# Copies and attention of the first batch a step later, in a kernel of top-k attention and Fourier mixing

## The chip, the cores and the metric

The kernel runs on one core of a Trainium2 chip. Its time is the device time of one execution in microseconds; the time before is the median of three runs. A core has five engines that run side by side and wait for each other by semaphores: TensorE (PE, with its weight loads as PEld), VectorE (DVE), ScalarE (ACT), GpSimd (POOL) and SyncE (SP), which issues transfers here. [...]

## What is computed

There are 8 batches with 8 heads, 576 tokens and a head size of 64. For each row of the scores, only the 32 largest stay, and the softmax is taken over them; its product with v is the attention's output. Per batch, the heads side by side make a 576 x 512 matrix x. It is mixed by a Fourier transform over both axes, normalised, and sent through two layers of weights:

```python
scores = scale * np.matmul(q, k.transpose(0, 1, 3, 2))
kth = np.partition(scores, -top_k, axis=-1)[..., -top_k:-top_k + 1]
scores = np.where(scores >= kth, scores, -1000000000.0)
...
mixed = np.real(np.fft.fft(np.fft.fft(x, axis=1), axis=2))
u = x + mixed
un = (u - mu) / np.sqrt(var + 1e-06)
return u + np.maximum(un @ w_ch1, 0.0) @ w_ch2
```

The weights arrive as 64-bit floats. The kernel reads them as pairs of 32-bit words and makes 32-bit floats of them itself.

## The kernel before

**Items and steps.** Two heads make a pair, four pairs a batch. The rows of a pair's scores are cut into nine items (`IN_PAIR`, L301): four row tiles of 128 for each head, and one item (e is None) with the 64 last rows of both heads. The main loop (L1394) has one step per item, 36 for a batch (`PER_BATCH`). Steps 1 to 36 are those of the first batch's items (`short`, L1399), in which no layer of the batch before can run yet.

**One item's way.** Its scores are made on TensorE three steps ahead (`scores`, L309: a large product of 128 x 512 per head, L369, and a small one for the last keys, L339), and ScalarE copies them to the tile S at once (L372, L343). VectorE finds the 32 largest in four rounds of MAX8 (L393) with three MATCH_REPLACE8 (L395) between. GpSimd makes two thresholds of them (`bounds`, L402). ScalarE's mask (L409) and a GpSimd subtraction (L412) turn the scores into what the exponential (L418, `expo`) needs. A step later TensorE transposes the result P in blocks of 128 (`transposes`, L439, L450) and ScalarE copies the blocks to PT (L442, L451). When a few items are there, `attend` (L476) multiplies PT with v; `attended` (L490, L502) copies the output and the sums; `to_tokens` (L516) transposes it back, and VectorE normalises it into x (L520).

**The weights.** During steps 1 to 33 of the first batch, 32 chunks of weights of 128 x 512 are converted, about one per step: ScalarE scales the high word (L191), converts the low word (L207) and takes the sign (L210); VectorE shifts the result by three bits (L199); GpSimd adds the low word (L218) and multiplies by the sign (L220). The plan (`at`, L1212) calls the ScalarE part "convert", the others "shift", "join" and "pool". Four column means of the first weights are taken on TensorE (`centre`, L1246, L1250), in steps 19, 27, 36 and 37; their copy by ScalarE (L1263) is under "convert" of the step after. GpSimd then subtracts them (L1259): for the first two one instruction in each of the four steps that follow.

**Order in a step.** It is written out by hand. ScalarE first runs "convert", then the exponential of the item before; then the list `fixed` is worked through: scores with their copies, query or key transposes for the next pair (`prep`, L269), attention's tokens, planned TensorE work, transposes of P with their copies, attention. Then the loads are issued on SyncE (`load_nat`, `load_v`), and VectorE's rounds, GpSimd's thresholds and the mask of the step's own item follow. In step 36 the attention of the last items is finished, and step 37 has VectorE fold x for the Fourier products (L631 to L586); the products over tokens (`dft_tokens`, L667), over channels (L724, L728) and the first layer (L878) follow.

**Buffers.** Score products and column means share two banks (`ps_s`); query, key and P transposes share two others (`ps_t`); attention and its tokens have one (`ps_o`), other work three (`ps_m`). A bank is free again when the copy out of it is done.

```python
        fixed.append(lambda: scores(j - 1, 1) if e == 1 else scores(j, 0))
        fixed += preps
...
            fixed.append(lambda: transposes(done))
...
        run(i, "convert")
        if short:
            expo(i - 1)
        for n, fn in enumerate(fixed):
            cost += fn()
...
        if i < PER_BATCH:
            mask(i, lambda: run(i, "join"))
```

Of the kernel before, what the change touches and what calls it, by code (L numbers as in the profile page):

```python
# [18 lines left out]
P = 128  # L19
# [53 lines left out]
def kernel(  # L73
# [234 lines left out]

    def scores(i, part):  # L309

# [21 lines left out]
        if part == 1:  # L332

            copy = nc.scalar.copy if i else nc.vector.tensor_copy
            shape, name = [P, NF * P], f"sp_{i}_t"
            sp = ps_s.tile(shape, F32, name=name, tag="sp") if i else bank(shape, name)

            q_end = P * t + rows
            nc.tensor.matmul(  # L339
                sp[:, 0:P], lhsT=qT[:, q_end - P:q_end], rhs=kt_t, start=True, stop=True  # L340
            )
            for h, (s_t, r, _, tails) in enumerate(to):
                copy(out=s_t[r, tails], in_=sp[P - rows:P, TAIL * h:TAIL * (h + 1)])  # L343
            return 0.3
        if e is None and i >= PER_BATCH:

            half = NF * P // 2
            sps = [
                ps_s.tile([P, NF * P], F32, name=f"sp_{i}_{h}", tag="sp") for h in range(2)
            ]  # L350
            for g in range(2):
                for h in range(2):
                    hd = slice(D * h, D * (h + 1))
                    nc.tensor.matmul(
                        sps[h][TAIL * g:TAIL * (g + 1), 0:half],
                        lhsT=qT[hd, q_cols], rhs=kT[hd, half * g:half * (g + 1)],
                        start=True, stop=True,
                    )
            for h, (s_t, r, _, _) in enumerate(to):
                for g in range(2):  # L360
                    nc.scalar.copy(
                        out=s_t[r, half * g:half * (g + 1)],
                        in_=sps[h][TAIL * g:TAIL * (g + 1), 0:half],
                    )
            return 0.6
        for h, (s_t, r, keys, _) in enumerate(to):
            hd = slice(D * h, D * (h + 1))
            sp = ps_s.tile([P, NF * P], F32, name=f"sp_{i}_{h}", tag="sp")
            nc.tensor.matmul(  # L369
                sp[r], lhsT=qT[hd, q_cols], rhs=kT[hd, :], start=True, stop=True  # L370
            )
            nc.scalar.copy(out=s_t[r, keys], in_=sp[r])  # L372
        return 1.04
# [48 lines left out]

    def transposes(i):

# [4 lines left out]
        if (pair, ch) not in PT:  # L429
            PT[pair, ch] = attp.tile(  # L430
                [P, 2 * NF + 1, CW[ch]], F32, name=f"PT_{pair}_{ch}", tag=f"PT{ch}", bufs=1
            )
        pt = PT[pair, ch]

        def full():
# [5 lines left out]
            for he, o, w in dsts:  # L441
                nc.scalar.copy(  # L442
                    out=pt[:, NF * he:NF * (he + 1), col:col + w], in_=tp[:, :, o:o + w]
                )

        def tails():
            tp = ps_t.tile([P, 4, P], F32, name=f"tpP_{i}_t", tag="tp")
            if e == 1:
                both = Wp.pop(i - 1).rearrange("p e s -> p (e s)")[:, NF * P:S + TAIL]
                nc.tensor.transpose(tp[:, 0, :], both, ident)  # L450
                nc.scalar.copy(out=pt[:, 2 * NF, col:col + P], in_=tp[:, 0, :])  # L451
                return
            Wp.pop(i)
            nc.tensor.transpose(tp[:, 0, :], p_sb[:, S - P:S], ident)
            nc.scalar.copy(out=pt[TAIL:P, 2 * NF, col:col + TAIL], in_=tp[TAIL:P, 0, TAIL:P])
            for r in (0, TH):
                nc.scalar.copy(
                    out=pt[r:r + TH, 2 * NF, col:col + TAIL],
# [892 lines left out]

    queue, waiting, pending, written, now, out_next = [], [], [], set(), [0], []
    step_us = 6.0

# [39 lines left out]
    while i < N + 4 or plan or queue or sums:  # L1394
# [9 lines left out]
        fixed, j = [], i + 3  # L1404
        e = items[j][2] if j < N else None
        preps = []
# [21 lines left out]
        for where in ("pe1", "pe2", "pe"):  # L1428
            fixed += plan.pop((i, where), [])
        if e is None and j < N:  # L1430
            fixed.append(lambda: scores(j, 1))
        n_tr = len(fixed)
        if done is not None:
            fixed.append(lambda: transposes(done))
        if short:
            fixed += tok
            pair, r = divmod(i - 1, PER_PAIR)
            piece = {1: (0, 0, P), 4: (0, P, CW[0]), 6: (1, 0, P), 8: (1, P, CW[1])}.get(r)
            if piece is not None:
                fixed.append(lambda: attend(pair, *piece))  # L1440
            if i == PER_BATCH:
                fixed.append(lambda: attended(NPB - 1, 1, late_next) or 0.0)
                fixed.append(lambda: to_tokens(NPB - 1, 1, False))
        if i in arrivals:
# [21 lines left out]
        if short:  # L1466
            if piece is not None and r in (4, 8) and i < PER_BATCH:

# [82 lines left out]
```

## Time and profile before

| | |
|---|---|
| time, median of three runs | 1907.32 us (1907.11 to 1907.42) |
| the profiled execution: its own time / span | 1907.16 us / 1905.4 us |
| TensorE busy, whole span | 1790.4 us (94%) |
| VectorE busy, whole span | 1585.3 us (83%) |
| ScalarE / GpSimd busy, whole span | 1208.5 / 908.4 us |
| mean granted TensorE clock | 0.969 |
| step of the first batch, between two threshold products (L402) | 5.42 us with a shift, 5.08 without |
| last threshold product of the first batch begins | 217.63 us |
| first product of the first layer (L878) begins | 255.88 us |

The span runs from the first to the last instruction; the execution's own time has a little more around it. A row of the timeline has start and duration in us, engine, line, operation, output<-inputs, shapes and count, and in brackets how long the engine had stood idle before it and what ended that. Where stretches are compared, each row has the stretch, its length, each engine's busy time in us with its count of instructions, the granted TensorE clock as a share of full speed, and the share of the DMA engines. Times from L402 mean: counted from the start of that item's threshold product.

### The profile page before, as it was taken

The numbers are of one execution on the slowest core, as the hardware profiler recorded it, in microseconds if no ns is written. First come the engines' busy times: TensorE is split into PE (matmuls) and PEld (weight loads), VectorE is DVE, ScalarE is ACT, GpSimd is POOL, SyncE is SP. The second block draws the span as 40 slices with busy tenths as digits, with TensorE's granted clock in tenths as the row PEclk, the third lists the DMA queues.
The fourth block names the chain that finished last, engine by engine and source line by source line (L and its number), as shares of the span: only waits on it lengthen the run. The fifth ranks groups of instructions, "written<-read, shape, count | busy, mean of one in ns | idle before, by whom it ended". The sixth has DMA issues, their size and how long they took to land.

```text
span 1905.4 us, 28704 instructions
## 1 busy us (share of the span) xinstructions
PE 1790.4 (94%) x9200; PEld 1182.4 (62%) x9200; DVE 1585.3 (83%) x3301; ACT 1208.5 (63%) x3078; POOL 908.4 (48%) x1278
## 2 busy tenths in 40 slices
PE   5567799999899999999999999999999999999999
PEld 3344465474567756667567656667567656667678
DVE  7999999999899999989899888989899888872110
ACT  6878657776766767657676667666676667652100
POOL 4768643556535374345534464245534464241022
PEclk7787899999999999999999999999999999999999
DMA  5333001311104111131113101141113102030132
GB/s 165 104 94 108 20 13 50 99 56 25 41 14 130 34 25 47 42 107 28 25 47 98 53 20 52 35 114 27 25 47 97 53 19 57 25 103 6 50 101 80
DMA packets 184342, 111.25 MB, mean 58 GB/s; under 512 B 125952, under 2 KB 174208, under 8 KB 184192
## 3 DMA queue, kind: packets, MB, share of 16 engines
q1 hardware_dynamic: 183408, 109.20, 20.3%
q8 instruction: 74, 1.21, 0.3%
q14 instruction: 76, 0.62, 0.1%
q10 hardware_dynamic: 784, 0.21, 0.0%
HBM read 93.63 MB, written 15.73 MB: 57 GB/s over the span
## 4 chain that ended last, share of the span: by engine, by line
PE 80%; ACT 8%; DVE 6%; POOL 3%; issue 1%; DMA 1%; SPq 1%; POOLq 0%; DVEq 0%; ACTq 0%
PE hp L878 26%; PE cp L905 10%; PE o L476 8%; PE tpP L439 6%; PE sp L369 5%; PE cw L1075 5%; PE cv L1075 4%; PE yp L667 3%; PE cp L944 3%; DVE m L393 2%; DVE wk L395 2%; PE sp_t L339 2%; PE mp L728 2%; POOL wk L412 1%; ACT wk L409 1%
## 5 line engine op out<-in xcount | busy, mean ns | idle before, releaser
L412 POOL TENSOR_TENSOR wk<-S,wk 128x576 f32<-128x576 f32 x288 | 407.7, 1416 | 731.8 <-ACT wk L409 701.2
L393 DVE MAX8 m<-wk 128x8 f32<-128x576 f32 x864 | 626.3, 749 | 6.1
L878 PE MATMUL hp<-unT,w 128*128 128x256 f32 (+1 forms) x2048 | 539.9, 410 | 2.6 <-ACT unT L796 2.6
L878 PEld LDWEIGHTS hp<-unT,w 128*128 128x128 f32 x2048 | 374.3, 191 | 124.7 <-issue 25.8
L395 DVE MATCH_REPLACE8 wk<-m,wk 128x576 f32<-128x576 f32 x576 | 427.6, 742 | 0.0
L418 ACT ACTIVATE wk<-wk,nt 128x576 f32<-128x576 f32 x288 | 224.7, 780 | 75.6 <-POOL wk L412 74.5
L409 ACT ACTIVATE wk<-S,nt 128x576 f32<-128x576 f32 x288 | 226.8, 787 | 36.2 <-POOL nt L402 35.2
L439 PE MATMUL tpP<-ident,wk 128*128 128x128 f32 x1152 | 183.9, 284 | 67.3 <-ACT wk L418 40.7
L905 PE MATMUL cp<-w,hT 128*128 128x512 f32 x512 | 240.6, 598 | 0.0
L442 ACT COPY PT<-tpP 128x512 f32<-128x512 f32 (+1 forms) x320 | 171.2, 547 | 106.8 <-PE tpP L439 104.3
L393 DVE MAX8 m<-S 128x8 f32<-128x576 f32 x288 | 214.0, 743 | 21.6 <-ACT S L343 21.6
L439 PEld LDWEIGHTS tpP<-ident,wk 128*128 128x128 f32 x1152 | 141.2, 145 | 141.2 <-ACT wk L418 64.2
L882 ACT ACTIVATE hT<-hp 128x320 f32<-128x320 f32 (+1 forms) x256 | 104.7, 409 | 194.5 <-PE hp L878 192.1
L395 DVE MATCH_REPLACE8 wk<-m,S 128x576 f32<-128x576 f32 x288 | 213.7, 742 | 0.0
L476 PE MATMUL o<-PT,v 128*64 128x256 f32 (+3 forms) x1440 | 195.2, 414 | 1.9 <-ACT PT L442 1.8
L372 ACT COPY S<-sp 128x512 f32<-128x512 f32 (+1 forms) x264 | 141.7, 588 | 48.9 <-PE sp L369 48.6
L369 PE MATMUL sp<-kT,qT 64*128 64x512 f32 (+1 forms) x528 | 160.2, 666 | 4.8 <-ACT means L1263 3.3
L476 PEld LDWEIGHTS o<-PT,v 128*64 128x64 f32 x1440 | 111.4, 152 | 73.8 <-issue 16.7
L905 PEld LDWEIGHTS cp<-w,hT 128*128 128x128 f32 x512 | 88.8, 190 | 86.3 <-issue 86.2
L1020 POOL TENSOR_TENSOR hT<-hT 128x512 f32<-128x512 f32 x64 | 81.4, 1275 | 100.3 <-ACT hT L882 88.6
L1075 PE MATMUL cw<-w,hT 128*128 128x256 f32 x448 | 106.7, 383 | 1.4 <-POOL nt L402 1.2
L1075 PEld LDWEIGHTS cw<-w,hT 128*128 128x128 f32 x448 | 81.4, 190 | 18.9 <-issue 5.2
(157 smaller groups left out, 2179.3 us busy)
## 6 DMA issues: line engine op xcount, KB each, us to landing
w<-w_parts SPq DMA_DIRECT2D x82, 512.0 KB, 4.4
space<-in_moe_w_ch_dram SPq DMA_DIRECT2D x32, 512.0 KB, 3.5
nat<-in_q_dram SPq DMA_DIRECT2D x128, 64.0 KB, 2.1
v<-in_v_dram SPq DMA_DIRECT2D x128, 64.0 KB, 2.2
out_dram<-x SPq DMA_DIRECT2D x32, 256.0 KB, 2.1
nat<-in_k_dram SPq DMA_DIRECT2D x124, 64.0 KB, 2.2
w_parts<-w_t SPq DMA_DIRECT2D x8, 512.0 KB, 2.9
w_s<-w_parts SPq DMA_DIRECT2D x8, 512.0 KB, 4.8
```

Source lines behind the costliest of these rows:

```text
L369: nc.tensor.matmul(sp[r], lhsT=qT[hd, q_cols], rhs=kT[hd, :], start=True, stop=True)
L393: ops.append(lambda src=src, m8=m8: nc.vector.max(out=m8, in_=src))
L395: ops.append(lambda src=src, m8=m8: nc.vector.match_replace(w, m8, src, NEG))
L409: nc.scalar.activation(out=w, in_=Ssb[i], func=AF.Relu, scale=-FAR, bias=Nt[i][:, 1:2])
L412: nc.gpsimd.tensor_tensor(out=w, in0=Ssb.pop(i), in1=w, op=ALU.subtract)
L418: nc.scalar.activation(out=w, in_=w, func=AF.Exp, bias=Nt.pop(i)[:, 0:1], accum_out=den_t[pair % 3][:, c:c + 1],)
L439: nc.tensor.transpose(tp[:, c, :], p_sb[:, k0 + P * c:k0 + P * (c + 1)], ident)
L442: nc.scalar.copy(out=pt[:, NF * he:NF * (he + 1), col:col + w], in_=tp[:, :, o:o + w])
L476: nc.tensor.matmul(o[D * e:D * (e + 1), c0:c1], lhsT=vv[:, c, e, :], rhs=pt[:, 2 * NF if c == NF else NF * e + c, c0:c1], start=(c == 0), ...
L878: nc.tensor.matmul(hp[:, 0:w], lhsT=w1[:, dt, P * it:P * (it + 1)], rhs=unT[:, dt, 0:w], start=(dt == 0), stop=(dt == NDT - 1),)
L905: nc.tensor.matmul(cp, lhsT=hT[:, it, P * n:P * (n + 1)], rhs=w2[:, it, :], start=(it == 0), stop=(it == NIT - 1),)
L1075: nc.tensor.matmul(dst, lhsT=h()[a][:, kc, :], rhs=rhs_of(kc), start=start and kc == 0, stop=kc == NK - 1, skip_group_check=True,)
```

## The change

In the first batch:

- Scores of an item are made four steps ahead (`next_scores(i + 4, held_s)`), behind the transposes of P, and their copies are kept in a list and issued at the beginning of ScalarE's next step. An item with e None makes its three score products in one step.
- The copies of P are kept likewise (`held`) and issued a step later, ahead of the exponential. Attention of an item's group runs a step later, after the scores; its tokens follow it.
- ScalarE's step begins with the scaling ("scale", L191 alone) and ends, ahead of the mask, with the rest of "convert" (L207, L210, and the copy of a column mean).
- The exponential stands in the list, behind the copies, the query or key transposes and the planned TensorE work, ahead of the transposes of P.
- In step 36 everything that ends the batch goes first: exponential, copies, transposes, attention, its copy and tokens; the held score copies, planned work (the third column mean) and the query transposes come after.

```diff
+    def copier(held):
+        if held is None:
+            return nc.scalar.copy
+        return lambda **kw: held.append(lambda: nc.scalar.copy(**kw))
...
-            nc.scalar.copy(out=s_t[r, keys], in_=sp[r])
+            copier(held)(out=s_t[r, keys], in_=sp[r])
...
-    def transposes(i):
+    def transposes(i, held=None):
...
+        copy = copier(held)
...
-        at(s0 + 1, "convert", lambda n=n: scale_high(n))
+        at(s0 + 1, "scale", lambda n=n: scale_high(n))
...
-        fixed.append(lambda: scores(j - 1, 1) if e == 1 else scores(j, 0))
+
+        def next_scores(j, held=None):
+            if e_of(j) == 1:
+                return scores(j - 1, 1, held)
+            t = scores(j, 0, held)
+            return t + scores(j, 1, held) if e_of(j) is None and held is not None else t
+
+        if 1 < i <= PER_BATCH:
+            begun_s = held_s[:]
+            held_s.clear()
+            fixed.append(lambda: [fn() for fn in begun_s] and 0.0)
+        else:
+            fixed.append(lambda: next_scores(j))
         n_mask = 0
-        fixed += preps
+        if i != PER_BATCH:
+            fixed += preps
...
-        if done is not None:
+        if done is not None and not short:
             fixed.append(lambda: transposes(done))
         if short:
-            fixed += tok
-            pair, r = divmod(i - 1, PER_PAIR)
+            begun = held[:]
+            held.clear()
+            last_of = i == PER_BATCH
+
+            def copies():
+                for fn in begun:
+                    fn()
+                return 0.0
+
+            tile = i - 1 if last_of else i - 2
+            pair, r = divmod(tile, PER_PAIR)
             piece = {1: (0, 0, P), 4: (0, P, CW[0]), 6: (1, 0, P), 8: (1, P, CW[1])}.get(r)
...
+            if last_of:
+                fixed[:] = [
+                    lambda: expo(i - 1) or 0.0, copies, lambda: transposes(i - 1), *pieces,
+                    lambda: attended(NPB - 1, 1, late_next) or 0.0,
+                    lambda: to_tokens(NPB - 1, 1, False), *fixed, *preps,
+                ]
+            else:
+                fixed.insert(1, copies)
+                fixed += [
+                    lambda: expo(i - 1) or 0.0, lambda: transposes(i - 1, held),
+                    lambda: next_scores(i + 4, held_s), *pieces, *tok,
+                    lambda: run(i, "convert") or 0.0,
+                ]
...
-        run(i, "convert")
-        if short:
-            expo(i - 1)
+        run(i, "scale")
+        if not short or last_of:
+            run(i, "convert")
```

More of the change, by code (lines that the diff above doesn't have):

```diff
@@ L307, with scores @@
     N = len(items)
-    def scores(i, part):
+    def copier(held):
+        if held is None:
+            return nc.scalar.copy
+        return lambda **kw: held.append(lambda: nc.scalar.copy(**kw))
+    def scores(i, part, held=None):
         if not 0 <= i < N:
@@ L332, in scores @@
         if part == 1:
-            copy = nc.scalar.copy if i else nc.vector.tensor_copy
+            copy = copier(held) if i else nc.vector.tensor_copy
             shape, name = [P, NF * P], f"sp_{i}_t"
@@ L360, in scores @@
                 for g in range(2):
-                    nc.scalar.copy(
+                    copier(held)(
                         out=s_t[r, half * g:half * (g + 1)],
@@ L441, in full @@
             for he, o, w in dsts:
-                nc.scalar.copy(
+                copy(
                     out=pt[:, NF * he:NF * (he + 1), col:col + w], in_=tp[:, :, o:o + w]
@@ L450, in tails @@
                 nc.tensor.transpose(tp[:, 0, :], both, ident)
-                nc.scalar.copy(out=pt[:, 2 * NF, col:col + P], in_=tp[:, 0, :])
+                copy(out=pt[:, 2 * NF, col:col + P], in_=tp[:, 0, :])
                 return
@@ L454, in tails @@
             nc.tensor.transpose(tp[:, 0, :], p_sb[:, S - P:S], ident)
-            nc.scalar.copy(out=pt[TAIL:P, 2 * NF, col:col + TAIL], in_=tp[TAIL:P, 0, TAIL:P])
+            copy(out=pt[TAIL:P, 2 * NF, col:col + TAIL], in_=tp[TAIL:P, 0, TAIL:P])
             for r in (0, TH):
-                nc.scalar.copy(
+                copy(
                     out=pt[r:r + TH, 2 * NF, col:col + TAIL],
@@ L1352 @@
     queue, waiting, pending, written, now, out_next = [], [], [], set(), [0], []
+    held, held_s = [], []
     step_us = 6.0
@@ L1404, with e_of @@
         fixed, j = [], i + 3
-        e = items[j][2] if j < N else None
+        def e_of(j):
+            return items[j][2] if j < N else None
+        e = e_of(j)
         preps = []
@@ L1429 @@
             fixed += plan.pop((i, where), [])
-        if e is None and j < N:
+        if e is None and j < N and not 1 < i <= PER_BATCH:
             fixed.append(lambda: scores(j, 1))
         n_tr = len(fixed)
-        if done is not None:
+        if done is not None and not short:
             fixed.append(lambda: transposes(done))
         if short:
-            fixed += tok
-            pair, r = divmod(i - 1, PER_PAIR)
-            piece = {1: (0, 0, P), 4: (0, P, CW[0]), 6: (1, 0, P), 8: (1, P, CW[1])}.get(r)
[L1439 to L1443, printed above, removed]
+            begun = held[:]
[7 more added lines that the diff above has]
+            pair, r = divmod(tile, PER_PAIR)
+            piece = {1: (0, 0, P), 4: (0, P, CW[0]), 6: (1, 0, P), 8: (1, P, CW[1])}.get(r)
+            piece = piece if tile >= 0 else None
+            pieces = [lambda: attend(pair, *piece)] if piece is not None else []
+            if last_of:
[11 more added lines that the diff above has]
+                ]
         if i in arrivals:
@@ L1466 @@
         if short:
-            if piece is not None and r in (4, 8) and i < PER_BATCH:
+            if piece is not None and r in (4, 8) and not last_of:
                 out_next.append(lambda pc=(pair, r // 8): attended(*pc, late_next))
```

## The prediction, made before the result was known

> **What bounds the kernel now.** I read the stages first (busy time of each engine in four stretches), then the one VectorE group of the first batch whose durations differ from one another, then the timeline around it, and last the timeline where the first batch ends. All rows are of the profiled execution (span 1905.4 us, own time 1907.16 us; the median of the runs is 1907.32 us, so a sum against this execution carries over to the median within 0.2 us).
>
> ```profile
> core 0: us, PE busy (x) PEld busy (x) DVE busy (x) ACT busy (x) POOL busy (x), PEclk, DMA share, GB/s
> 17.00:120.00 103.00, 63.47 (x327) 41.87 (x329) 101.48 (x209) 87.79 (x204) 73.46 (x71) 0.72 0.42 127
> 120.00:217.60 97.60, 65.82 (x323) 39.20 (x322) 94.89 (x193) 79.25 (x185) 76.98 (x72) 0.78 0.25 75
> 217.60:255.90 38.30, 32.42 (x208) 21.45 (x206) 37.22 (x88) 18.25 (x49) 12.06 (x28) 1.00 0.04 9
> 255.90:1905.00 1649.10, 1620.01 (x8321) 1076.20 (x8321) 1343.85 (x2789) 1017.49 (x2628) 744.55 (x1100) 1.00 0.19 53
> ```
>
> VectorE is busy 98.5% and 97.2% of the first batch and 97.2% of the change to the second, TensorE 98.2% of all that follows. So the change, which touches only the first batch, can act in two ways: VectorE's time up to 217.6 us, and the moment at which TensorE begins its unbroken work after 255.9 us. What is won or lost there shifts the end by as much, for what follows keeps its order and waits for no clock.
>
> VectorE hardly waits in the first batch. What it loses lies inside its own instructions, in the integer shift of a weight chunk (L199):
>
> ```profile
> L199 DVE TENSOR_SCALAR w<-w x32: 401/411/1403, 21.8 to 206.3; 128x512 int32<-128x512 int32 x32
> ```
>
> The group's busy time is 19.5 us where 32 times 0.41 would be 13.1: 6.4 us are stretching, in 11 of the 32 shifts. There is also one true wait, of 1.3 us (L199 for ScalarE's L191). One stretched shift in the timeline:
>
> ```profile
> 74.59 0.78 ACT L409 ACTIVATE wk<-S,nt 128x576 f32<-128x576 f32 x1
> ...
> 75.45 1.43 POOL L412 TENSOR_TENSOR wk<-S,wk 128x576 f32<-128x576 f32 x1 [1.65 <-ACT wk L409]
> ...
> 76.83 1.29 POOL L220 TENSOR_TENSOR w<-w,space 128x512 f32<-128x512 f32 x1
> ...
> 77.38 1.02 DVE L199 TENSOR_SCALAR w<-w 128x512 int32<-128x512 int32 x1
> ```
>
> The shift begins while GpSimd multiplies (76.83 to 78.12) and ends 0.28 us after it. GpSimd was late since ScalarE's mask (L409) was late: it began 2.46 us after the threshold product (L402, at 72.13) that it needs. A full step of VectorE is 5.42 us from one L402 to the next, and the next shift starts 5.26 us after it. Mask to L412 is 0.86, L412 to the end of L220 2.68. So a mask later than 5.26 - 2.68 - 0.86 = **1.72 us** after its L402 stretches the next shift, by as much as it is later, up to about 1.1.
>
> Then the end of the batch, on TensorE:
>
> ```profile
> 217.74 0.98 PE L283 MATMUL tpq<-ident,nat 128*128 128x128 f32 x5
> 218.56 3.60 PE L1250 MATMUL cm<-w,ones 128*128 128x512 f32 x8
> 222.15 0.66 PE L439 MATMUL tpP<-ident,wk 128*128 128x128 f32 x4
> ...
> 225.25 0.44 PE L516 MATMUL tpx<-ident,xT 128*128 128x128 f32 x2 [0.46 <-ACT xT L490]
> 225.62 0.87 PE L354 MATMUL sp<-kT,qT 64*64 64x256 f32 x8
> 227.32 3.70 PE L1250 MATMUL cm<-w,ones 128*128 128x512 f32 x8 [0.84 <-ACT S L361]
> ...
> 234.30 0.75 PE L667 MATMUL yp<-fs,fg 128*64 128x145 f32 x7
> ```
>
> The query transposes and the third column mean fill the 4.4 us in which TensorE would wait for the last softmax. Later it waits for VectorE's folds just once, so its slack there is 1.15 us:
>
> ```profile
> 239.83 0.46 PE L667 MATMUL yp<-fs,fsp 128*64 128x145 f32 x2 [1.15 <-DVE fsp L563]
> ```
>
> [...] 0.41 us for 512 elements alone, up to 1.40 beside GpSimd, ending 0.28 after GpSimd's instruction. [...] So a copy that waits holds the mask behind it; the 1.3 us wait is such a case (ScalarE stood 2.92 us for a score copy behind the first column mean).
>
> **The change part by part.** No instruction is added or removed; the order views of GpSimd and SyncE are the same row by row, those of TensorE, ScalarE and VectorE differ only up to the batch's end. VectorE's difference is each normalisation a step later: nothing, as it has no wait there and its inputs come a step earlier than it.
>
> *Copies of P and scores a step later, scaling first, conversion last.* ScalarE's step becomes: scaling (L191), score copies, copies of P, query or key copies, exponential, L207 and L210, mask. It no longer waits for transposes or scores of its own step. In a plain step, counted from L402: mask at 0.33, L191 at 1.02, copies from 1.58 to 3.0 (two score copies 0.94, one of P 0.48), exponential when GpSimd's L412 is done, 0.33 + 0.86 + 1.5 = 2.7 or 3.13 behind L218, 0.87 for it, 1.12 for the two conversions: free at 5.13, the next mask wanted at 5.75. So a plain step has 0.62 + 1.39 = 2.0 us before a shift is stretched. That removes the plain cases (32.7, 54.6, 77.4, 105.6 us: 1.9 us in all) and the 1.3 us wait.
>
> *New waits.* (a) Key or query copies follow their transposes (0.98 at full clock, 1.33 at half) in ScalarE's order, ahead of the exponential; the copy of attention's output stands right behind the score copies, while attention is now TensorE's last work of the step before. For the latter, from L402 of step 6 of a pair: transposes to 0.7, tail scores to 1.15, 192 columns of attention 2.2 to 3.9 us (between the rows at full and at half clock), so it ends at 3.4 to 5.1, where ScalarE arrives at 2.5. With 1.0 for the copies of output and sums, 0.48 for P, 0.87 and 1.12, the mask comes 1.5 to 3.2 late: 0 to 1.2 us of stretching after the limit of 1.72. The query step of the pair comes out alike. Eight such places at about 0.5: 4.1 us. (b) Scores held over a step need banks, of which there are two. The order with its waits shows a third score tile (items 13, 22) and, where a column mean holds a bank (items 23 to 24 and 31), the second one too, waiting on TensorE for a copy in ScalarE's next step, with attention queued behind it at items 23 to 24. That makes ScalarE some 4.5 us late in steps 20 and 28: 0.9 each in the shift after, 1.8. (c) Steps 20 to 23 and 28 to 31 give GpSimd a fourth long instruction (L1259): 0.37 + 1.26 + 1.38 + 1.30 + 1.33 = 5.64 against VectorE's 5.42, so the shift meets it whatever ScalarE does: 8 times 0.22 = 1.8. Sum left: 4.1 + 1.8 + 1.8 = 7.7 us, against 6.4 + 1.3 = 7.7 before. **The first batch gains nothing.** The bounds are 2.1 us left (only c and a little), a gain of 5.6, and 11.7 (every place of a at its upper end), a loss of 4.
>
> *The last step.* Attention goes first; score copies, the third column mean and the query transposes come behind it. Counted from the last tile's L402 (217.63): exponential at 0.65 + 0.85 + 1.5 = 3.0, transposes of P at 3.9 (4.5 before), the output's transposes end 3.54 later as before, at 7.5; then the column mean, 3.6, to 11.0; the first query transposes 0.7; their copies 0.7; the mean's copy, behind them on ScalarE, 0.6, to 13.0; the scores that wait for its bank 0.7. The copies of those scores (L361) begin at 13.7; before, at 226.53 - 217.63 = 8.9. From there to the first Fourier products all is as before, a chain of two banks: **4.8 us later**. Of that the 1.15 us of slack hide some; 3.65 are left. VectorE, with its folds done, then waits for the products' sums (L734), so it brings nothing back. The cover lost is the wait for the last softmax, which hid 4.4 us of this. SyncE's key load behind the query transposes starts some 10 us later, five steps before it is used: nothing.
>
> Sum: 1907.16 + 0 + 3.65 = 1910.8, with the median's 0.16 more **1911.0 us**.
>
> **Rivals.** *Copies come off cleanly (0.25):* TensorE's clock is mostly full, attention ends in 2.2 us, and only c is left. For it: ScalarE's 2.0 us of margin. Against it: the clock of 0.72 to 0.78. Gain 5.6, loss 3.65: 1905.4; this one is not slower. It decides where masks stay under 1.72 us after L402. *The same, and the end of the batch is covered too (0.08):* 1901.7; against it speaks the chain of two banks. *ScalarE falls behind (0.17):* every stall of a at half clock, the 4 us loss with 3.65: 1914.9. *The forecast (0.50)* spans 1908.5 to 1913.5.
>
> **How the numbers follow.** The measurement tells 0.2%, 3.8 us, from no change. Slower by more: half of the forecast, 0.25, all of the third rival, 0.17, with rounding 0.43. Faster by more: the second rival and a fifth of the first, 0.13. The same: 0.44. The range, 1903.5 to 1915.5, leaves out most of the second rival and the tail of the third.
>
> **What would show it.** Right: L199's busy time after near 19 us, in steps with key, query or output copies and from step 20; ScalarE idle before output and query copies; L361's group starting 13 to 14 us after the last tile's L402; VectorE idle some 3 us before the first L734. Wrong: L199 near 15 us in sum, or no idle VectorE after the folds.

## The result, and the profile after

The changed kernel takes **1919.92 us** (median of five runs, 1916.47 to 1925.49), the kernel before beside it 1907.32 us: a ratio of 1.0071, with a 95% interval of 1.005 to 1.0093. The forecast was 1911.0, with a range up to 1915.5. The profiled execution of the changed kernel took 1916.47 us, with a span of 1914.7 us. The added lines move line numbers by 5 or 6: L402 is now L407, L409 is L414, L412 is L417, L418 is L423, and held copies of scores and P are all L312.

The stages first, cut where the events of before lie now: the last threshold product of the first batch (224.76 us, before 217.63) and the first product of the first layer (268.84 us, before 255.88). The columns are those of the table in the prediction.

```profile
17.00:120.00 103.00, 61.23 (x306) 37.77 (x306) 101.49 (x210) 83.89 (x194) 70.88 (x69) 0.67 0.41 123
120.00:224.70 104.70, 66.00 (x312) 39.38 (x314) 96.50 (x189) 81.51 (x189) 79.01 (x73) 0.71 0.25 73
224.70:268.80 44.10, 37.17 (x237) 24.46 (x233) 38.83 (x90) 20.58 (x54) 10.80 (x28) 0.94 0.03 8
268.80:1914.50 1645.70, 1615.35 (x8321) 1073.32 (x8321) 1343.97 (x2789) 1017.16 (x2628) 744.84 (x1100) 1.00 0.19 53
```

The second stretch is 7.1 us longer, the third 5.8 us (44.1 for 38.3), and VectorE's share of them falls to 92% and 88%. Together 12.96 us are lost before the first layer. The last stretch is 3.6 us shorter, though no instruction in it changed: TensorE's half-clock time in it is 3.4 us here and 13.7 us in the profiled execution of before. That costs half of the difference, 5.1 us, if all work takes twice as long at half clock: an estimate, at its upper end (four transposes of P, L439 in the profile of before, took 0.66 us at full clock and 1.12 at half). So the loss to compare with the medians (12.6 us) is the 13.0 us at the first layer.

VectorE's group of shifts (busy time, mean ns | idle time just before them, and what ended it), with ScalarE's and GpSimd's longest waits up to 270 us (total, times, longest):

```profile
L199 DVE TENSOR_SCALAR w<-w 128x512 int32<-128x512 int32 x32 | 21.2, 662 | 6.9 <-ACT w L191 6.9
```

```profile
ACT S L312 <- PE sp L374: 16.7, 16, 2.7
ACT xT L496 <- PE o L482: 12.4, 8, 2.3
...
POOL w L218 <- ACT space L207: 42.0, 23, 4.3
```

Stretching of the shifts is 21.2 - 13.1 = 8.1 us (before 6.4), and VectorE now also waits 6.9 us for L191 itself (before 1.3): 15.0 us lost in the first batch, where the forecast had 7.7. ScalarE's wait for attention (L482) was 1.2 us in all before. One such place in the timeline:

```profile
54.38 0.41 DVE L199 TENSOR_SCALAR w<-w 128x512 int32<-128x512 int32 x1
...
54.82 0.42 ACT L496 COPY xT<-o 128x320 f32<-128x320 f32 x1 [2.32 <-PE o L482]
...
56.26 0.78 ACT L423 ACTIVATE wk<-wk,nt 128x576 f32<-128x576 f32 x1
...
57.03 0.68 ACT L207 ACTIVATE space<-space 128x512 int32<-128x512 uint32 x1
...
57.79 1.30 POOL L218 TENSOR_TENSOR w<-w,space 128x512 int32<-128x512 int32 x1 [2.95 <-ACT space L207]
...
59.05 1.41 POOL L417 TENSOR_TENSOR wk<-S,wk 128x576 f32<-128x576 f32 x1
...
59.80 0.93 DVE L199 TENSOR_SCALAR w<-w 128x512 int32<-128x512 int32 x1
...
60.41 1.47 POOL L220 TENSOR_TENSOR w<-w,space 128x512 f32<-128x512 f32 x1
```

ScalarE stands 2.32 us before the output copy, since attention is TensorE's last work of the step before. The exponential behind it is late, L207 behind that is late, GpSimd stands 2.95 us for L207, and the next shift begins while GpSimd subtracts (L417, until 60.46 us) and ends some 0.3 us after that: 0.93 us instead of 0.41.

VectorE's four waits for L191 end at 123.6, 137.6, 187.9 and 195.2 us. The first stands behind query copies, the third behind score copies that wait for TensorE while a column mean holds one of the two score banks (its copy begins only at 186.06 us):

```profile
116.31 2.40 PE L482 MATMUL o<-PT,v 128*64 128x128 f32 x20
118.64 1.33 PE L283 MATMUL tpq<-ident,nat 128*128 128x128 f32 x5
119.79 0.71 ACT L291 ACTIVATE qT<-tpq 128x512 f32<-128x512 f32 x2 [2.56 <-PE tpq L283]
...
123.63 1.22 DVE L199 TENSOR_SCALAR w<-w 128x512 int32<-128x512 int32 x1 [0.93 <-ACT w L191]
...
180.21 0.58 ACT L312 COPY S<-sp 64x512 f32<-64x512 f32 x1 [1.32 <-PE sp L374]
...
181.95 0.58 ACT L312 COPY S<-sp 64x512 f32<-64x512 f32 x1 [1.16 <-PE sp L374]
...
187.90 1.18 DVE L199 TENSOR_SCALAR w<-w 128x512 int32<-128x512 int32 x1 [2.68 <-ACT w L191]
```

The second (2.23 us) is of the kind of the third, with an output copy behind it; the fourth (1.07 us) stands behind an output copy (1.75 us of wait), one step after the third. So the loss is not spread evenly. The group of shifts up to 120 us and from there on:

```profile
L199 DVE TENSOR_SCALAR w<-w 128x512 int32<-128x512 int32 x17 | 8.6, 507 | 0.0
L199 DVE TENSOR_SCALAR w<-w 128x512 int32<-128x512 int32 x15 | 12.6, 839 | 6.9 <-ACT w L191 6.9
```

With 0.41 us for a shift, 1.6 us are lost up to 120 us and 13.4 us behind it. Two kernels of the next section whose edits do not touch these steps, e1 and (up to step 30) e14, show the same two large waits in their profiles: 2.24 us near 138 us, and 3.67 and 2.40 us near 190 us. They lose 1.9 and 2.3 us up to 120 us, 16.8 and 14.1 us behind it.

The end of the batch on TensorE:

```profile
231.63 1.12 PE L445 MATMUL tpP<-ident,wk 128*128 128x128 f32 x4
...
235.19 0.44 PE L522 MATMUL tpx<-ident,xT 128*128 128x128 f32 x2 [0.46 <-ACT xT L496]
235.47 3.60 PE L1256 MATMUL cm<-w,ones 128*128 128x512 f32 x8
238.90 0.71 PE L283 MATMUL tpq<-ident,nat 128*128 128x128 f32 x5
...
249.25 0.72 PE L673 MATMUL yp<-fs,fg 128*64 128x145 f32 x8
```

The mean and the query transposes now lie behind attention, in the open. The mask of the last tile begins 3.64 us after its L407 (before 0.59), so its transposes begin 6.9 us after it (before 4.5).

### The profile page after: what moved, and what is told of

The parts are those of the page before. It is cut to its first block, busy times and chain, and to the rows that moved or that the text cites. A ratio compares the mean times of both kernels' runs of the same rounds, so it can differ in the third digit from the quotient of the medians.

```text
span 1914.7 us, 28695 instructions
## 1 busy us (share of the span) xinstructions
PE 1788.7 (93%) x9200; PEld 1178.8 (62%) x9200; DVE 1588.6 (83%) x3301; ACT 1208.8 (63%) x3078; POOL 906.8 (47%) x1278
## 4 chain that ended last, share of the span: by engine, by line
PE 82%; ACT 8%; DVE 5%; POOL 3%; issue 1%; DMA 1%; SPq 0%; POOLq 0%; DVEq 0%; ACTq 0%
PE hp L884 26%; PE cp L911 10%; PE o L482 9%; PE sp L374 6%; PE tpP L445 6%; PE cw L1081 5%; PE cv L1081 4%; PE yp L673 3%; PE cp L950 3%; DVE m L398 2%; PE sp_t L344 2%; DVE wk L400 2%; ACT wk L423 2%; PE mp L734 2%; POOL wk L417 1%
## 5 line engine op out<-in xcount | busy, mean ns | idle before, releaser
L417 POOL TENSOR_TENSOR wk<-S,wk 128x576 f32<-128x576 f32 x288 | 407.3, 1414 | 718.0 <-ACT wk L414 700.9
L423 ACT ACTIVATE wk<-wk,nt 128x576 f32<-128x576 f32 x288 | 225.2, 782 | 70.8 <-POOL wk L417 69.0
L414 ACT ACTIVATE wk<-S,nt 128x576 f32<-128x576 f32 x288 | 226.4, 786 | 36.1 <-POOL nt L407 35.2
L448 ACT COPY PT<-tpP 128x512 f32<-128x512 f32 (+1 forms) x281 | 150.4, 547 | 92.3 <-PE tpP L445 90.0
L482 PE MATMUL o<-PT,v 128*64 128x256 f32 (+3 forms) x1440 | 187.9, 412 | 0.1
L374 PE MATMUL sp<-kT,qT 64*128 64x512 f32 (+1 forms) x528 | 168.9, 698 | 3.5 <-ACT S L312 1.3
L482 PEld LDWEIGHTS o<-PT,v 128*64 128x64 f32 x1440 | 106.1, 152 | 77.1 <-issue 25.0
L377 ACT COPY S<-sp 128x512 f32<-128x512 f32 (+1 forms) x226 | 121.2, 589 | 44.6 <-PE sp L374 44.5
```

What stands on the lines that cost most here:

```text
L374: nc.tensor.matmul(sp[r], lhsT=qT[hd, q_cols], rhs=kT[hd, :], start=True, stop=True)
L414: nc.scalar.activation(out=w, in_=Ssb[i], func=AF.Relu, scale=-FAR, bias=Nt[i][:, 1:2])
L417: nc.gpsimd.tensor_tensor(out=w, in0=Ssb.pop(i), in1=w, op=ALU.subtract)
L423: nc.scalar.activation(out=w, in_=w, func=AF.Exp, bias=Nt.pop(i)[:, 0:1], accum_out=den_t[pair % 3][:, c:c + 1],)
L448: copy(out=pt[:, NF * he:NF * (he + 1), col:col + w], in_=tp[:, :, o:o + w])
L482: nc.tensor.matmul(o[D * e:D * (e + 1), c0:c1], lhsT=vv[:, c, e, :], rhs=pt[:, 2 * NF if c == NF else NF * e + c, c0:c1], start=(c == 0), ...
```

## The experiments

My theory after the result: ScalarE's first copies of a step wait for TensorE's last work of the step before, at half clock (the granted clock was 0.67 and 0.71 on the mean) for longer than a step can absorb. Rivals: conversion at the end of ScalarE's step, the banks that held scores need, the reordered step 36, TensorE's clock alone. For each kernel the table gives the ratio to the kernel before (run beside it), and from its profile: VectorE's loss in the shifts (busy time of L199 less 13.1, plus its wait for L191), the last threshold product of the batch, and the first product of the first layer.

| kernel | ratio (95% interval) | loss, us | last threshold product | first layer |
|---|---|---|---|---|
| before | 1 | 6.4 + 1.3 = 7.7 | 217.63 | 255.88 |
| changed | 1.0071 (1.005 to 1.0093) | 8.1 + 6.9 = 15.0 | 224.76 | 268.84 |
| e1, end undone | 1.0077 (1.0065 to 1.009) | 9.7 + 8.9 = 18.6 | 228.89 | 271.48 |
| e2, end alone | 1.0011 (1.0004 to 1.0017) | 4.7 + 1.3 = 6.0 | 215.91 | 257.38 |
| e3, scaling first alone | 1.0151 (1.0137 to 1.0164) | 16.7 + 17.7 = 34.4 | 245.97 | 285.29 |
| e4, scores as before | 1.0155 (1.0137 to 1.0172) | 16.0 + 13.6 = 29.6 | 242.59 | 287.97 |
| e5, conversion first | 1.0054 (1.0042 to 1.0066) | 9.1 + 0.3 = 9.4 | 220.48 | 264.80 |
| e6, output copy late | 1.0009 (1.0003 to 1.0016) | 5.8 + 1.8 = 7.6 | 216.96 | 257.15 |
| e7, e5 and end undone | 1.0053 (1.0039 to 1.0068) | 8.4 + 0.3 = 8.7 | 221.34 | 265.03 |
| e8, warm | 1.0017 (1.001 to 1.0023) | 4.5 + 5.3 = 9.8 | 219.22 | 262.12 |
| e9, means in own banks | 1.0049 (1.0035 to 1.0063) | 9.7 + 1.7 = 11.4 | 222.20 | 266.24 |
| e10, e6 and e9 | 0.9995 (0.9987 to 1.0003) | 3.5 + 0.0 = 3.5 | 212.81 | 255.88 |
| e11, exponential ahead of held copies | 0.9976 (0.9966 to 0.9985) | 3.4 + 0.0 = 3.4 | 212.58 | 253.86 |
| e12, before, warm | 1.003 (1.0019 to 1.0042) | 8.1 + 3.3 = 11.4 | 221.35 | 260.43 |
| e13, e11, third mean early | 0.9969 (0.9957 to 0.9981) | 2.7 + 0.0 = 2.7 | 211.93 | 251.15 |
| e14, changed, third mean early | 1.0062 (1.0047 to 1.0077) | 10.7 + 5.7 = 16.4 | 226.28 | 267.78 |
| e15, before, third mean early | 1.0001 (0.9993 to 1.0009) | 5.2 + 1.8 = 7.0 | 217.27 | 258.13 |
| e16, e11, both means early | 0.9973 (0.9965 to 0.9982) | 2.7 + 0.0 = 2.7 | 211.68 | 251.34 |

The ratio follows the last column: 13.0 us at the first layer are 0.68% of 1907 us (measured 0.71), 1.3 us of e6 0.07% (0.09), 29.4 us of e3 1.54% (1.51); the farthest off is e8, with 0.33% (0.17). The loss column is that of one execution each, and chance in it is up to some 4 us: e2 does not touch the first batch ahead of step 36 and shows 1.7 us less than before; e1 does not either and shows 3.6 us more than the changed kernel.

**e1, e2: the order of step 36, undone in the changed kernel and done alone.**

```diff
-                    lambda: expo(i - 1) or 0.0, copies, lambda: transposes(i - 1), *pieces,
-                    lambda: attended(NPB - 1, 1, late_next) or 0.0,
-                    lambda: to_tokens(NPB - 1, 1, False), *fixed, *preps,
+                    lambda: expo(i - 1) or 0.0, fixed[0], copies, *preps, *fixed[1:],
+                    lambda: transposes(i - 1), *pieces,
+                    lambda: attended(NPB - 1, 1, late_next) or 0.0,
+                    lambda: to_tokens(NPB - 1, 1, False),
```

> The changed kernel with only the order of step 36 as before (score copies, query transposes and third column mean ahead of the last transposes and attention). Theory of the loop (ScalarE's first copies of a step wait for TensorE's last work of the step before, so the first batch itself is 7 us longer): the last threshold product of the batch stays near 224.8 us (before 217.6), and only the part of the end goes: some 4 us less than the changed kernel's 1919.9, about 1916. Rival, the reordered end is the cause of most of it: about 1908. The forecast's own sum: 3.65 less.

e2, in the kernel before:

```diff
+        if i == PER_BATCH:
+            fixed[:] = fixed[n_tr:] + fixed[:n_tr]
```

> The kernel before with only step 36 reordered: last transposes, attention, its output first, then scores, query transposes and third column mean. Forecast's sum: the first batch is untouched (last threshold product at 217.6), L361's copies come 4.8 us later, 1.15 are hidden: 1907.3 + 3.65 = 1911. Rival, the end is most of the loss: 1916 or more. If the end is covered: 1907.

e2 bears the forecast's step out. The score copies that it priced, in the timeline of e2:

```profile
230.02 1.51 ACT L361 COPY S<-sp 64x256 f32<-64x256 f32 x4 [0.75 <-PE sp L354]
```

They begin 14.1 us after the last threshold product (forecast 13.7, before 8.9), and the way from there to the first layer is 41.5 us instead of 38.3: 3.2 us, against 3.65. The total is 2 us up (0.8 to 3.2 by the interval). But e1 gains nothing, so the end is not where most of the loss is, and undoing its order does not bring its price back. The rival is out.

**e3, e5, e7: where the conversion stands.** e3 changes the kernel before in nothing else:

```diff
-        run(i, "convert")
+        run(i, "scale")
+        if not short or i == PER_BATCH:
+            run(i, "convert")
...
         if short:
+            run(i, "convert")
```

> The kernel before with only ScalarE's order of weight work changed: scaling first, low word and sign last, ahead of the mask; scores, copies of P and attention as before. Theory of the loop: no wait is closed into a loop, so the first batch is within 2 us of before, 1905 to 1909. Rival, conversion at the end of ScalarE's step makes GpSimd late and is the cause: 1912 or more, with GpSimd waiting tens of us for L207.

My theory fails here, and clearly: 1.5% slower. The timeline of e3 shows a closed chain across GpSimd and TensorE:

```profile
97.25 0.78 ACT L418 ACTIVATE wk<-wk,nt 128x576 f32<-128x576 f32 x1 [0.99 <-POOL wk L412]
...
98.17 1.11 PE L439 MATMUL tpP<-ident,wk 128*128 128x128 f32 x4 [3.82 <-ACT wk L418]
99.32 0.59 ACT L442 COPY PT<-tpP 128x512 f32<-128x512 f32 x1 [0.25 <-PE tpP L439]
...
99.96 0.69 ACT L207 ACTIVATE space<-space 128x512 int32<-128x512 uint32 x1
...
100.73 1.29 POOL L218 TENSOR_TENSOR w<-w,space 128x512 int32<-128x512 int32 x1 [1.94 <-ACT space L207]
...
103.41 0.78 ACT L418 ACTIVATE wk<-wk,nt 128x576 f32<-128x576 f32 x1 [0.98 <-POOL wk L412]
```

Exponential, transposes, their copy, L207, L218, subtraction, next exponential: 6.16 us a round, where VectorE's step is 5.42. In the changed kernel the copy of P is a step later and so out of this chain; what is left of it there (from the place shown above: exponential to L207 0.77, L207 to L218 0.76, L218 to L417 1.26, L417 1.41) is 4.2 us. A round absorbs at most 1.2 us of lateness; in the place shown it was 0.7, since ScalarE has its other copies to make as well: the next exponential begins at 60.99 us, 4.73 us after the one at 56.26. So I added this chain to the theory and put the conversion back to the front, with the new end (e5) and the old one (e7):

```diff
-        if not short or last_of:
-            run(i, "convert")
+        run(i, "convert")
...
-                    lambda: run(i, "convert") or 0.0,
```

> The changed kernel with the rest of the weight conversion (L207, L210) again right behind the scaling at the beginning of ScalarE's step; held copies, delayed attention and reordered end stay. Theory of two loops (scaling-only start closes the chain L207, L218, subtraction, exponential, L207, and leaves TensorE's products of the last step too little time before ScalarE's copies): both loops get 1.1 us or more of slack, the last threshold product of the batch comes at 218 us or earlier (changed kernel 224.8), and the total is 1907 to 1911. Rival, the held copies and the delayed attention are the cause whatever stands behind them: 1917 to 1922.

> The changed kernel with conversion first and step 36 in its old order: held copies and delayed attention alone. Theory of two loops: first batch as in e5, the end 2 us cheaper (what the reordered end alone cost the kernel before): 1904 to 1908. Rival, held copies cost by themselves: 1914 or more.

VectorE's waits for L191 go (6.9 to 0.3 us), but 9.1 us of stretching stay and the total is far above what I expected. The first layer begins 4.0 us earlier than in the changed kernel, but the intervals of the ratios overlap. The conversion's place decides mainly whether VectorE waits or is stretched; most of the loss has another cause. The end undone again gives nothing (e7 against e5).

**e4: scores three steps ahead and copied at once, the rest changed.**

```diff
-        if 1 < i <= PER_BATCH:
-            begun_s = held_s[:]
-            held_s.clear()
-            fixed.append(lambda: [fn() for fn in begun_s] and 0.0)
-        else:
-            fixed.append(lambda: next_scores(j))
+        fixed.append(lambda: scores(j - 1, 1) if e == 1 else scores(j, 0))
...
-                    lambda: next_scores(i + 4, held_s), *pieces, *tok,
+                    *pieces, *tok,
```

> The changed kernel with scores made three steps ahead and copied at once at the beginning of the step, as before; copies of P and attention still a step later, end reordered. Theory of the loop: ScalarE's first copies of a step now wait for scores that TensorE makes after the attention of the step before, so the loop is as long as in the changed kernel or longer: 1916 to 1924. Rival, the held score banks are the cause: first batch like before, 1911.

The direction is the theory's, the size twice as large: ScalarE waits some 60 us for scores that TensorE makes behind attention. So copying the scores at once is no cure; with the new order held scores are needed. What their banks cost is the question of e9.

**e6: the output copy behind the exponential.**

```diff
-                for fn in out_next:
-                    fn()
-                out_next.clear()
+                if not short or last_of:
+                    outputs()
...
-                    lambda: expo(i - 1) or 0.0, lambda: transposes(i - 1, held),
+                    lambda: expo(i - 1) or 0.0, outputs, lambda: transposes(i - 1, held),
```

> The changed kernel with the copies of attention's output and sums behind the exponential instead of behind the score copies. Term (a) of the forecast, the output copy waiting for attention (12.4 us of ScalarE's waits in the changed kernel), is the cause: last threshold product near 219, total 1911 to 1914. Theory of two loops with conversion last as the closing link: the wait moves to another copy, 1916 to 1920.

This one edit takes away 11.7 of the 13.0 us. The wait does not move to another copy. Shifts and ScalarE's waits of e6:

```profile
L199 DVE TENSOR_SCALAR w<-w 128x512 int32<-128x512 int32 x32 | 18.9, 591 | 1.8 <-ACT w L191 1.8
```

```profile
ACT S L312 <- PE sp L374: 14.6, 14, 2.6
...
ACT xT L496 <- PE o L482: 3.7, 6, 1.2
```

The waits of the held score copies are about as before the edit (16.7 and 14.6 us), so they do not make the difference; the output copies do. The edit moves some 1.0 us of copying per place along with the wait, so it does not tell the two apart. The loss is 7.6 us, what the forecast had for the whole change. Up to 120 us and behind it, the shifts of e6 are

```profile
L199 DVE TENSOR_SCALAR w<-w 128x512 int32<-128x512 int32 x17 | 7.9, 467 | 0.0
L199 DVE TENSOR_SCALAR w<-w 128x512 int32<-128x512 int32 x15 | 11.0, 731 | 1.8 <-ACT w L191 1.8
```

so only 0.7 us of the gain lie up to 120 us, where three output copies stand with no column mean near them. 6.7 us lie behind it, and 5.1 of these are waits of VectorE, which follow score and query copies as much as output copies. The last tile's exponential begins 2.5 us after its threshold product instead of 5.95, so the end is 3.9 us shorter too (40.2 us to the first layer instead of 44.1).

**e8, e12: TensorE kept busy.** Eight transposes of the identity per step, which nobody reads, where TensorE waits for the exponential (e8), or ahead of the transposes of P (e12):

```diff
+        def warm():
+            t = bank([P, 4, P], f"warm_{i}")
+            for n in range(8):
+                nc.tensor.transpose(t[:, n % 4, :], ident, ident)
+            return 0.0
...
-                    lambda: expo(i - 1) or 0.0, lambda: transposes(i - 1, held),
+                    lambda: expo(i - 1) or 0.0, warm, lambda: transposes(i - 1, held),
```

> The changed kernel with eight more TensorE transposes of the identity per step of the first batch, put where TensorE waits for the exponential; nobody reads them. If the half clock of TensorE is what makes ScalarE's first copies wait: the granted clock of the first batch rises from 0.67 to 0.71 towards 0.85 or more, the copies' waits shrink, and the total falls to 1908 to 1914. If the order alone is the cause: 1919 or more, since they only add 0.9 us of TensorE work per step.

> The kernel before with the same eight idle transposes per step as in the warmed changed kernel, put ahead of the transposes of P. The kernel before has slack for TensorE, so the clock is worth little: within 3 us of the kernel before, between 1904 and 1909, though the granted clock of the first batch rises from 0.75 to 0.85 or more. If the clock is what costs in either kernel: 1902 or less.

The first two stages of e8:

```profile
17.00:120.00 103.00, 69.89 (x463) 48.92 (x464) 101.49 (x213) 89.73 (x206) 74.34 (x72) 0.86 0.40 127
120.00:219.20 99.20, 71.90 (x442) 46.90 (x440) 92.59 (x187) 76.87 (x180) 75.24 (x71) 0.89 0.24 74
```

With a granted clock of 0.86 and 0.89 (0.67 and 0.71 without) and more TensorE work, the changed kernel is some 10 us faster by the ratio, 6.7 us at the first layer. VectorE's remaining waits, 5.3 us, lie at 132, 182 and 190 us alone, behind the column means. So half clock carries a part of the loss, and the waits behind the means outlast it. In the kernel before the same work costs 0.3%, more than I expected: there the copies of P wait for transposes of their own step, which it delays (ScalarE's wait for L439 rises from 21.7 to 25.0 us; that this is the whole of it was not tested). The edit adds work as well as clock, so it does not give the clock's price by itself.

**e9, e10: the first two column means in banks of their own.**

```diff
-        cm = ps_s.tile([P, DM], F32, name=f"cm_{c}", tag="sp")
+        shape, name = [P, DM], f"cm_{c}"
+        cm = bank(shape, name) if early else ps_s.tile(shape, F32, name=name, tag="sp")
```

> The changed kernel with the first two column means in banks of their own instead of the two that scores use. If the bank that a column mean holds (steps 20 and 28, term (b) of the forecast) makes ScalarE late beyond what a step can absorb: VectorE's waits for L191 (6.9 us, all at 122 to 195 us) go, total 1911 to 1915. If the output copy waiting for attention is enough by itself: VectorE's waits stay above 4 us and the total at 1916 or more.

> The changed kernel with both: output copies behind the exponential, and the two column means in banks of their own. Both causes gone: VectorE's waits under 0.5 us, L199 near 16 us in sum, last threshold product at 214 to 215 us, total 1903 to 1905 (the end's 2 us included). If the banks are nothing: as with the output copy alone, 1.0009 times the kernel before.

The means' banks are a second cause: 3.6 us of the loss in the changed kernel and 4.1 beside e6 (7.6 to 3.5). Each is a difference of single executions, and in e9 the total falls less clearly (the intervals of e9 and the changed kernel overlap); beside e6 the ratio falls from 1.0009 to 0.9995. With both out VectorE never waits in the batch; of the 3.5 us left, 2.8 lie between 132 and 197 us, where GpSimd has its fourth long instruction. The two causes act in the same stretch: behind 120 us the loss is 13.4 us in the changed kernel, 6.6 in e6, 7.3 in e9 and 2.9 in e10. Of the 4.1 us that e10 gains on e6 in the batch, 1.3 are left at the first layer: in its profiled execution TensorE's granted clock from 217.6 to 256 us was 0.92, in e6 it was 1.00. What that cost was not shown.

**e11: ScalarE's old step with the held copies behind the exponential**, the output copies behind those, the means of e9 and the old step 36:

```diff
-                fixed.insert(1, copies)
+                fixed[:1] = [lambda: expo(i - 1) or 0.0, fixed[0], copies]
                 fixed += [
-                    lambda: expo(i - 1) or 0.0, lambda: transposes(i - 1, held),
+                    lambda: transposes(i - 1, held),
                     lambda: next_scores(i + 4, held_s), *pieces, *tok,
-                    lambda: run(i, "convert") or 0.0,
                 ]
```

> The changed kernel with ScalarE's step as in the kernel before (scaling and conversion, then the exponential), the held copies of scores and P behind the exponential, output copies behind those, column means in own banks, step 36 in its old order. If what counts is that no copy that waits for the step before stands ahead of the exponential: L199 near 15 us in sum, no wait of VectorE, total 1901 to 1905, faster than both kernels. Rival: held copies behind the exponential make the mask late as before, 1906 to 1908.

It beats both kernels, 0.9976. Its loss is that of e10 (3.4 and 3.5 us), though key and query copies stand behind the exponential here and ahead of it there. With the output copies and the banks out of the way those four pairs of copies cost at most the 0.7 us that e10 loses outside 132 to 197 us. In company it was otherwise: in the changed kernel the query copies at 119.79 us stand ahead of a wait of 0.93 us.

**e13 to e16: what carries the end.** e11 is 5 us ahead at the last threshold product, but starts its Fourier products at 234.3 us, as the kernel before. In its timeline TensorE has attention of step 35 (2.4 us), query transposes and the third mean (4.0 us) in a row up to 222.2 us. The third mean was put into step 31 and a bank of its own (e13, e14, e15), in e16 the fourth into step 34 as well. The edit of e13 to e15 begins:

```diff
-            start_of[n1] + 2 + 8 * c if early else PER_BATCH - 2 + c, "pe",
+            start_of[n1] + 2 + 8 * c if early else (31 if c == 2 else PER_BATCH - 2 + c), "pe",
```

> The version with the exponential ahead of the held copies (e11), with the third column mean made in step 31, in a bank of its own, instead of step 36. If TensorE's queue sets the end of the batch (the mean took 4.0 us at 218.3 us, with the last exponential done at 216.6): the first Fourier product starts some 4 us earlier, at 230 to 231 us, and the total is 1896 to 1899. If the mean costs as much in step 31 as in step 36: 1901, as e11.

> The changed kernel with the third column mean made in step 31 in a bank of its own; step 36 keeps its new order. If the mean behind attention is what the new order costs at the end: 3 to 4 us less than the changed kernel, 1915 to 1917. If step 31 has no room for it, since ScalarE's first copies already wait for TensorE there: 1919 or more.

> The kernel before with the third column mean made in step 31 in a bank of its own. Before, the mean stood where TensorE waited for the last softmax, so its place was nearly free, and behind it the products waited for VectorE's folds (1.15 us): within 2 us of before, 1904 to 1908. If TensorE's queue bounded the end before as well: 1901 to 1903.

> As e13, and the fourth column mean made in step 34 instead of step 37. If TensorE's queue is all that stands between the last exponential and the Fourier products: another 3.7 us less than e13, 1893 to 1896. If VectorE's folds of x come to bound the products, as they did for 1.15 us before: the same as e13 within 2 us, with TensorE waiting for the folds.

e13 starts its products 4.7 us earlier (229.6) and its first layer 2.7 us earlier; the ratios of e11, e13 and e16 overlap. In e16 the bound has become VectorE's folds, as the rival said:

```profile
229.83 1.60 PE L673 MATMUL yp<-fs,fg 128*64 128x145 f32 x7 [3.77 <-DVE fg L569]
```

e14 is no different from the changed kernel: it has 41.5 us from the last threshold product to the first layer instead of 44.1, but that product comes 1.5 us later. e15 stays within 0.1% of before, for a reason that I had not expected. In its profile, with the mean gone, TensorE idles 3.57 us, the clock falls to half from 220.9 to 234.5 us (0.65 on the mean from 217 to 230 us, 1.00 in the kernel before), and the next mean takes 6.60 us (3.70 in the kernel before):

```profile
221.41 1.12 PE L439 MATMUL tpP<-ident,wk 128*128 128x128 f32 x4 [3.57 <-ACT qT L291]
...
228.66 6.60 PE L1252 MATMUL cm<-w,ones 128*128 128x512 f32 x8 [0.85 <-ACT S L361]
```

## Why the prediction was wrong

**The failing step** is the way in which terms (a) and (b) were priced: "the mask comes 1.5 to 3.2 late: 0 to 1.2 us of stretching after the limit of 1.72 [...] Eight such places at about 0.5: 4.1 us", and "some 4.5 us late in steps 20 and 28: 0.9 each in the shift after, 1.8". Each late mask was taken alone, and its whole price was what the one shift after it can stretch. A wait of VectorE for L191 stands in the sum at nothing. The places and the waits were right: ScalarE stands before the output copies, the query copies and the score copies behind a column mean, and late masks stretch shifts. Up to 120 us, with the output copies of steps 7, 11 and 16, even the size was about right: the loss is 1.6 us (1.9 in e1, 2.3 in e14). Behind 120 us, where column means, query and output copies follow each other within a few steps, it is 13.4 us (16.8 and 14.1).

The lines of the sum in its own terms, from the runs: the output copies cost 15.0 - 7.6 = 7.4 us in the batch (e6) and 3.9 us more at the end, the banks 4.1 us beside that (e6 to e10), and 3.5 us are left, of which up to 2.8 are (c). The forecast had 4.1 for all of (a), 1.8 for (b) and 1.8 for (c).

What the working missed is that lateness is carried over to the next step. ScalarE's queue goes on with what it owes, and with L207 behind the exponential a round of L207, L218, subtraction and exponential needs 4.2 of 5.42 us, so at most 1.2 us are made good a step. What is beyond goes to the next L191, for which VectorE waits outright: 6.9 us, of which 4.9 end at 137.6 and 187.9 us behind the means, 0.9 behind the query copies and 1.1 behind an output copy. Each of the edits e5, e6 and e9 alone takes most of this away (to 0.3, 1.8 and 1.7 us), which fits several late copies in a row better than one kind of copy alone. That these waits follow from the carried lateness is read from the timeline and fits e5 (L207 out of the round, the waits gone); how the rest of e5's 9.4 us comes about was only argued.

**Point by point.**
- *A plain step is clean:* right; no shift before 59 us is stretched in the changed kernel (before, two are). But L199's busy time is 21.2 us in all, not near 19.
- *(b), the banks, 1.8 us:* right in place (VectorE's waits that end at 137.6 and 187.9 us), too small: 3.6 to 4.1 us.
- *"The query step of the pair comes out alike":* in the changed kernel it does (123.63 us: 0.93 us of wait, 0.81 of stretching); with the output copies and banks out of the way it costs nearly nothing (e10).
- *(c), GpSimd's fourth instruction, 1.8 us:* about right; at most 2.8 us remain there when (a) and (b) are out (e10).
- *"Conversion last" at no price of its own:* wrong. e3 shows what it can cost (1.5%) when a copy that waits for the same step is left ahead of it. The forecast counted ScalarE's time, not the chain through GpSimd.
- *The last step, +3.65 us:* right for the order alone at the first layer (3.2 us, e2; 2 us in the total). In the changed kernel it is 5.8 us, since the last tile's mask is 3 us late. That undoing it gives nothing (e1, e7) the forecast did not see: attention of step 35 a step later fills TensorE ahead of the mean in either order. This reading rests on the timeline of e11; e13 supports it only in part.
- *VectorE idle some 3 us before the first sums of products:* 1.4 us (L740).
- *The rival "ScalarE falls behind", 1914.9:* the right one, and it too stopped at stretching.
- *Clock:* the forecast priced attention between full and half clock and took the middle. With the clock at 0.86 and 0.89 the loss is 9.8 us, at 0.67 and 0.71 it is 15.0 (e8). That the mean of two ends is no estimate, since at half clock the waits pass what a step absorbs, is an argument that no run tests.

## What to carry to other kernels

When copies are put off by a step, what matters is where they stand in the queue of the engine that makes them: a copy whose producer was the last work of the step before belongs behind, not ahead of, the operation that the next engines wait for (e6 moves one kind of copy and takes away most of the loss). Price a wait on an engine that has a cycle with others by the spare time of that cycle per step, not by what the first victim can stretch, and look for places where several such waits follow each other within a few steps. Test parts of a change alone and in place: here the conversion's place alone cost 1.5% (e3), and in company some 4 us at the first layer (e5).

## What the runs showed of the hardware

- The shift and GpSimd: of the 64 shifts (L199, 128x512) in the profiles of the kernel before and of the changed one, 39 took 0.40 to 0.43 us and 25 took 0.56 to 1.40. Each of the 25 began while GpSimd ran one of its long instructions (L412, L220 and L1259, in the changed kernel L417 and L220) and ended 0.28 to 0.29 us after it.
- A copy that waited held back what stood behind it on ScalarE: in the changed kernel the exponential's input was done at 116.94 us (L417, 115.52 + 1.42). ScalarE then stood 2.56 us for the query transposes, made the query copies from 119.79 us on, and began the exponential at 120.39.
- In the same two profiles TensorE's granted clock is either 1.00 or 0.50, and each stretch of one clock that is not cut off by the end of the record lasts 3.41 us or a whole multiple of it. Between 17 and 217 us I counted 116 windows of 3.41 us on the grid of those changes, by the profile's busy time. At full clock, all 24 windows with TensorE busy up to 45% were followed by half clock, though TensorE was idle for 95% or more of the window in only one of them; of the 22 busy 57% or more, one was. At half clock, full clock came back after 24 of 26 windows that were busy 90% or more, and after 1 of 33 that were busy less than 85%. That is what these two executions show; what sets the clock they do not tell.
- A little idle time reached far in e15. There the window with most of the 3.57 us of idle TensorE (from 217.5 us) was busy 10%; the three behind it were busy 84, 86 and 75% at half clock, and the clock stayed down until 234.5 us. The mean that began at 228.66 us took 6.60 us, in the kernel before, at full clock, 3.70.
- From the first layer on, the profiled executions take 1645.9 to 1651.2 us, the changed kernel 1645.9 and the kernel before 1649.5. Once half of their half-clock time there (3.4 and 13.7 us) is taken off, the estimate made with the result, the two take 1644.2 and 1642.7 us. So a part of the differences between single times fits how much half-clock time falls there, and the first batch is best compared at the first layer.
